# Linear attention and a gated MLP on one core: num of two pairs moved ahead, pair 0's 1/den spread alone, batch 2's transposes cut in four

## The chip, the cores and the metric

One core of a Trainium2 chip runs one program. The metric is device time in microseconds (us), as the median of a few executions. "Before" was run again in each set of experiments, on the same chip as the runs it is compared with; its median went from 302.92 to 303.43 us over five such sets, so differences of 0.3 us are read from traces, not from the times.

## The reference, cut to what matters

```python
def phi(x):
    return np.where(x > 0, x, np.exp(x) - 1.0) + 1.0
q_p, k_p = (phi(q), phi(k))                        # q, k, v: 8 batches, 8 heads, 576, 64
kv  = np.einsum('bhsd,bhse->bhde', k_p, v)
z   = np.sum(k_p, axis=2)
num = np.einsum('bhsd,bhde->bhse', q_p, kv)
den = np.einsum('bhsd,bhd->bhs', q_p, z)[..., None] + 1e-06
x   = num / den          # as 4608 tokens of 512
h   = x @ w_in           # 512 -> 2048
out = (h - np.tanh(h)) @ w_out
```

## The kernel before

Heads go in four pairs (two to the 128 partitions). The attention of batch b makes 576 tokens of x; the MLP works in nine tiles of 512 tokens, each a first layer (16 blocks of four 128x512 matmuls, each followed by tanh on ScalarE, ACT, and a subtraction on VectorE, DVE) and a second layer (16 steps of four). The attention of the next batches is put between these blocks, as little functions hung on block numbers (`s1` for the first layer, `s2` for the second). Batch 0 has nothing to hide behind. PSUM, where the tensor engine (PE) writes, is eight banks, handed out in a fixed rotation.

Names in the code and the profile lines: kp and qp are phi(k) and phi(q), qT is qp transposed; kz is kv times a mask, with the columns of z beside it; ns is num in SBUF (its "tail" is the last of the nine 64-token blocks of all pairs), rden is 1/den, and "spreading" means bringing rden to all 128 partitions; th is tanh(h), gT is h - th. "Dense" matmuls are those of the MLP.

The code is abridged; the last line is in words.

```python
def a_qT_pe(b, i, banks):                     # nine transposes of q, two banks, two copies
    ...
    for n, (j0, j1) in enumerate(((0, 5), (5, 9))):
        ps = banks()...
        for j in range(j0, j1):
            nc.tensor.transpose(ps[:, j - j0, :], ..., ident)
        if n == 0: nc.scalar.copy(dst, src)
        else:      nc.vector.tensor_copy(dst, src)

def a_num_copy(b, banks):                     # num to SBUF: the tail, then the pairs
    ns = rpool.tile(...)
    ps = num_mm(b, NP, banks)
    nc.scalar.copy(ns[:, :, 8, :], ps[:, 0:NP, :])
    if b == 0:
        for p in range(NP):
            num_mm(b, p, banks)
        for p in (0, 2):                      # two double copies
            nc.scalar.copy(ns[:, p:p + 2, 0:8, :]..., ps_all[:, 4 + p:6 + p, :])
    ...

# batch 0
a_qT_pe(0, 0, side); a_kv_half(0, 0, kvb)     # side: banks 4-7, kvb: banks 0-3
a_qT_pe(0, 1, side); a_kv_half(0, 1, kvb)
a_den(0, Banks([0]))                          # den on PE, 1/den on DVE
ns0 = a_num_copy(0, Banks([1, 4, 5, 6, 7]))
bp_a = a_spread_pe(0, 0, (0, 1))              # 1/den to 128 partitions, banks 0-3
bp_b = a_spread_pe(0, 4, (2, 3))              # banks 4-7
for p in range(NP):
    a_scale(0, p, ns0, (bp_a, bp_b)[p // 2], 144 * (p % 2))     # xT = num * (1/den)

# tile 0, second layer; tile 1, first layer (attn: banks 6, 7)
s2[14].append(lambda: a_qphi(2, 0)); s2[15].append(lambda: a_qphi(2, 1))
s1[1].append(lambda: a_kphi(2, 0))
s1[3].append(lambda: (a_kphi(2, 1), load_k(3), load_q(3)))
s1[5].append(lambda: a_qT_pe(2, 0, attn)); s1[7].append(lambda: a_qT_pe(2, 1, attn))
s1[9]: a_kv(2, attn)    s1[10]: load_v(4)    s1[11]: a_den, a_spread (1/den through DRAM: ds, then rdb)
```

## Time and profile before

| | before |
|---|---|
| time, median of 3 (then of 4) | 303.05 (302.92) us |
| span of the profiled execution | 301.5 us |
| TensorE (PE) busy | 97% |
| first dense matmul of tile 0 | 20.06 us |
| PE's waits at batch 2's transposes | 0.6 + 1.1 us |

As long as PE, busy for 97% of the time, is given the same work, the kernel gets faster only where PE stands still. The list of waits says where: in the chain of batch 0 before 20.06 us, and near 62 us. The lines are in the prediction.

### The profile page before, as it was taken

To read this page: it belongs to the slowest core of one execution; us is meant where nothing else is said; L and a number is where in the kernel's file an instruction comes from. 1 tells how busy PE (TensorE), PEld (TensorE's weight loads), DVE (VectorE), ACT (ScalarE), POOL (GpSimd) and SP (SyncE) were. 2 spreads that over 40 slices of the span, in tenths; PEclk is the share of its full clock that TensorE was granted. 3 is DMA by queue.
4 is the path that set the end of the run, shared out by engine and by line. 5 is a ranking of instruction groups with operands and counts; after the bars stand their busy time and mean duration, and the time that the engine had idled before them with its cause. 6 is when DMAs were issued, how large, how long until landed. Compare 5 with 4: busy or idle time off the path is not lost.

```text
span 301.5 us, 4703 instructions
## 1 busy us (share of the span) xinstructions
PE 292.2 (97%) x1790; PEld 138.7 (46%) x1790; DVE 180.0 (60%) x304; ACT 149.6 (50%) x228; POOL 51.7 (17%) x91
## 2 busy tenths in 40 slices
PE   8989999979999999999999999999999999999993
PEld 3544454444445444544454445444544444444441
DVE  7658944887557854785478556865681467008500
ACT  3637914954735653566256625662562166136420
POOL 8863253051006000600050003000000000000000
PEclk9999999999999999999999999999999999999998
DMA  6999999677879776967787777477108310130033
GB/s 95 193 206 206 205 207 206 171 113 139 214 101 188 147 170 139 152 109 200 142 145 128 192 149 125 85 177 148 38 2 193 71 35 0 37 86 18 2 70 70
DMA packets 36406, 38.23 MB, mean 127 GB/s; under 512 B 14432, under 2 KB 31008, under 8 KB 35616
## 3 DMA queue, kind: packets, MB, share of 16 engines
q0 software_dynamic: 17600, 18.35, 37.7%
q1 hardware_dynamic: 18784, 19.58, 28.9%
q8 instruction: 14, 0.23, 0.3%
q14 instruction: 8, 0.07, 0.1%
HBM read 43.78 MB, written 9.55 MB: 177 GB/s over the span
## 4 chain that ended last, share of the span: by engine, by line
PE 86%; DMA 4%; DVE 3%; ACT 2%; POOL 1%; issue 1%; SPq 0%; DVEq 0%; ACTq 0%; POOLq 0%
PE ps_all L275 39%; PE ps_all L290 38%; PE ps_all L165 4%; DMA out_dram<-osb 2%; PE ps_all L220 2%; DMA qraw<-in_q_dram 2%; ACT e L127 1%; DVE gT L281 1%; PE ps_all L190 1%; ACT osb L295 1%; PE ps_all L152 1%; POOL kraw L85 1%; PE ps_all L263 1%; DVE qp L129 1%; DVE kp L129 1%
## 5 line engine op out<-in xcount | busy, mean ns | idle before, releaser
L290 PE MATMUL ps_all<-w_out_sb,gT 128*128 128x512 bf16 x576 | 131.6, 379 | 0.0
L281 DVE TENSOR_TENSOR gT<-ps_all,th 128x512 bf16<-128x512 f32 x144 | 96.9, 687 | 53.6 <-ACT th L280 53.2
L275 PE MATMUL ps_all<-xT,w_in_sb 128*128 128x512 bf16 x576 | 128.2, 379 | 0.3 <-DVE xT L268 0.3
L280 ACT ACTIVATE th<-ps_all 128x512 f32<-128x512 f32 x144 | 85.2, 599 | 51.5 <-PE ps_all L275 46.8
L275 PEld LDWEIGHTS <-w_in_sb 128*128 128x128 bf16 x576 | 55.3, 98 | 66.6 <-issue 1.3
L290 PEld LDWEIGHTS <-gT 128*128 128x128 bf16 x576 | 55.6, 98 | 65.7 <-issue 0.3
L295 ACT COPY osb<-ps_all 128x512 f32<-128x512 f32 x36 | 21.1, 587 | 79.7 <-PE ps_all L290 59.6
L231 DVE TENSOR_TENSOR xT<-ps_all,rdb 128x512 bf16<-128x512 f32 x24 | 16.4, 689 | 11.8 <-PE ps_all L220 11.8
L104 POOL DMA_DIRECT2D v<-in_v_dram x32 | 19.2, 616 | 19.0 <-PE ps_all L165 6.0
L127 ACT ACTIVATE e<-kraw 128x1152 bf16<-128x1152 bf16 x16 | 18.5, 1165 | 5.3 <-DMA kraw<-in_k_dram 5.3
L129 DVE TENSOR_TENSOR kp<-e,r 128x1152 bf16<-128x1152 bf16 x16 | 12.2, 760 | 14.1 <-ACT e L127 13.0
L127 ACT ACTIVATE e<-qraw 128x1152 bf16<-128x1152 bf16 x16 | 18.4, 1166 | 0.6 <-DMA qraw<-in_q_dram 0.6
L129 DVE TENSOR_TENSOR qp<-e,r 128x1152 bf16<-128x1152 bf16 x16 | 12.1, 758 | 7.8 <-ACT e L127 7.0
L286 POOL COPY g<-gT 1x1 bf16<-1x1 bf16 x4 | 0.7, 176 | 92.9 <-DVE gT L281 92.9
L165 PE MATMUL ps_all<-v,kp 64*128 64x192 bf16 x288 | 13.7, 243 | 0.0
L165 PEld LDWEIGHTS <-kp 64*128 64x128 bf16 x288 | 11.5, 94 | 3.3 <-issue 2.5
L343 PE MATMUL ps_all<-zero 128*128 128x512 bf16 x36 | 10.3, 460 | 1.2 <-DVE zero L302 1.2
L220 PE MATMUL ps_all<-qT,kz 128*128 128x512 bf16 x32 | 11.2, 379 | 0.0
L89 POOL DMA_DIRECT2D kraw<-in_k_dram x14 | 8.7, 628 | 11.0 <-ACT th L280 9.6
L89 POOL DMA_DIRECT2D qraw<-in_q_dram x14 | 8.8, 642 | 6.1 <-DVE r L128 6.1
L268 DVE TENSOR_TENSOR xT<-ns,ps_all 128x576 bf16<-128x576 f32 x8 | 5.6, 749 | 5.2 <-PE ps_all L263 5.2
L174 DVE TENSOR_TENSOR kz<-ps_all,mask 128x320 bf16<-128x320 f32 x14 | 6.2, 486 | 3.7 <-PE ps_all L165 3.7
(46 smaller groups left out, 92.3 us busy)
## 6 DMA issues: line engine op xcount, KB each, us to landing
out_dram<-osb SPq DMA_DIRECT2D x72, 128.0 KB
rdb<-ds SPq DMA_DIRECT2D x12, 576.0 KB
v<-in_v_dram POOLq DMA_DIRECT2D x32, 144.0 KB, 6.4
kraw<-in_k_dram POOLq DMA_DIRECT2D x14, 288.0 KB, 5.1
qraw<-in_q_dram POOLq DMA_DIRECT2D x14, 288.0 KB, 7.0
w_in_sb<-in_moe_w_in_dram POOLq DMA_DIRECT2D x4, 512.0 KB, 10.1
w_out_sb<-in_moe_w_out_dram POOLq DMA_DIRECT2D x4, 512.0 KB, 13.2
kraw<-in_k_dram POOLq DMA_DIRECT2D x4, 144.0 KB, 3.7
```

The lines of the kernel that those rows point to most:

```text
L89: nc.gpsimd.dma_start(out=t[64 * hg:64 * hg + 64].rearrange("p i h j d -> p (i h) (j d)"), in_=src[b, 4 * hg:4 * hg + 4].rearrange("h (p j ...
L104: nc.gpsimd.dma_start(out=v_b[b % 2][64 * hg:64 * hg + 64, i, 0:2].rearrange("p h j d -> p h (j d)"), in_=v[b, h0:h0 + 2].rearrange("h (p ...
L127: nc.scalar.activation(e, x, AF.Exp)
L129: nc.vector.tensor_tensor(store[b][:, i].rearrange("p j h d -> p h j d"), e, r, ALU.min)
L165: nc.tensor.matmul(ps[hg], kp[r, i, j].rearrange("p h d -> p (h d)"), vt[r, i, :, j, :], start=(j == 0), stop=(j == J - 1))
L220: nc.tensor.matmul(ps, kz[:, p // 2, p % 2, 0:128], qT[:, p % 2, 0:8, p // 2, :], start=True, stop=True)
L231: nc.vector.tensor_mul(xT[:, p, S * b:S * b + 512].rearrange("p (j t c) -> p j t c", j=8, t=4), ps.rearrange("p j (t c) -> p j t c", t=4), ...
L275: nc.tensor.matmul(h, w_in_sb[:, p, fi * 128:(fi + 1) * 128], xT[:, p, c * 512:(c + 1) * 512], start=(p == 0), stop=(p == NP - 1))
L280: nc.scalar.activation(th, h, AF.Tanh)
L281: nc.vector.tensor_sub(gT[:, fi, :], h, th)
L290: nc.tensor.matmul(o, gT[:, fi, i * 128:(i + 1) * 128], w_out_sb[:, fi, :], start=(fi == 0), stop=(fi == NF - 1))
L295: nc.scalar.copy(osb, o)
```

## The change

Its intent: let ACT copy out half of batch 0's num early, let the first dense matmul wait for one scaled pair instead of two, and let the transposes of batch 2 flow between blocks instead of standing in a queue for two banks. The core of the diff (cut: num of batch 1, only rewritten in the same order, and the helpers):

```diff
     a_qT_pe(0, 1, side)
+    ns0 = new_ns(0)
+    for p in (0, 2):
+        a_num_copy(0, ns0, p, side)
     a_kv_half(0, 1, kvb)
     a_den(0, Banks([0]))
-    ns0 = a_num_copy(0, Banks([1, 4, 5, 6, 7]))
-    bp_a = a_spread_pe(0, 0, (0, 1))
-    bp_b = a_spread_pe(0, 4, (2, 3))
+    a_num_copy(0, ns0, NP, Banks([1]))
+    for p in (1, 3):
+        a_num_copy(0, ns0, p, side)
+    bp_a = a_spread_pe(0, 0, (0,))
+    bp_b = a_spread_pe(0, 4, (1, 2, 3))
     for p in range(NP):
-        a_scale(0, p, ns0, (bp_a, bp_b)[p // 2], 144 * (p % 2))
+        a_scale(0, p, ns0, bp_b if p else bp_a, 144 * (p - 1) if p else 0)
 ...
-            s1[5].append(lambda: a_qT_pe(2, 0, attn))
-            s1[7].append(lambda: a_qT_pe(2, 1, attn))
+            for n in range(4):
+                s1[4 + n].append(lambda n=n: a_qT_pe(2, n // 2, attn, (n % 2,)))
```

More of the change, by code (lines that the diff above doesn't have):

```diff
@@ L144, in a_qT_dma, with a_qT_pe @@
             in_=qp_t[b].rearrange("p i j h d -> p (i j h d)"))
-    def a_qT_pe(b, i, banks):
-        if i == 0:
+    def a_qT_pe(b, i, banks, parts=(0, 1)):
+        if i == 0 and 0 in parts:
             new_qT(b)
-        for n, (j0, j1) in enumerate(((0, 5), (5, 9))):
+        for n in parts:
+            j0, j1 = ((0, 5), (5, 9))[n]
             ps = banks().bitcast(BF16).rearrange("p (j t) -> p j t", t=128)
@@ L238, in a_num, with new_ns, a_num_copy @@
                 ps[:, 0:NP, :].rearrange("p a (t c) -> p a t c", t=4), rdb[:, :, :, 8, :])
-    def a_num_copy(b, banks):
-        ns = rpool.tile([128, NP, J, 64], F32, name="ns", tag="rdb")
-        ps = num_mm(b, NP, banks)
-        nc.scalar.copy(ns[:, :, 8, :], ps[:, 0:NP, :])
-        if b == 0:
-            for p in range(NP):
-                num_mm(b, p, banks)
-            for p in (0, 2):
-                nc.scalar.copy(ns[:, p:p + 2, 0:8, :].rearrange("p a j t -> p a (j t)"),
-                               ps_all[:, 4 + p:6 + p, :])
-        else:
-            for p in range(NP):
-                ps = num_mm(b, p, banks)
-                nc.scalar.copy(ns[:, p, 0:8, :], ps)
-        return ns
+    def new_ns(b):
+        return rpool.tile([128, NP, J, 64], F32, name="ns", tag="rdb")
+    def a_num_copy(b, ns, p, banks):
+        ps = num_mm(b, p, banks)
+        if p < NP:
+            nc.scalar.copy(ns[:, p, 0:8, :], ps)
+        else:
+            nc.scalar.copy(ns[:, :, 8, :], ps[:, 0:NP, :])
     def a_spread_pe(b, bank0, pairs):
@@ L384, with num1 @@
             s2[8].append(lambda: a_den(1, side))
-            s2[9].append(lambda: (sub.update(ns=a_num_copy(1, side)), load_v(3)))
+            def num1():
+                sub["ns"] = new_ns(1)
+                for p in (NP, 0, 1, 2, 3):
+                    a_num_copy(1, sub["ns"], p, side)
+                load_v(3)
+            s2[9].append(num1)
             s2[11].append(lambda: spread1(0))
```

## The prediction

> **What bounds the kernel now.** I read the page first: one busy engine, no throttling (the clock row is 9 throughout until the last slice), nothing slow in a row.
>
> ```profile
> PE 292.2 (97%) x1790; PEld 138.7 (46%) x1790; DVE 180.0 (60%) x304; ACT 149.6 (50%) x228; POOL 51.7 (17%) x91
> ```
>
> The tensor engine (PE) is nearly always occupied, so only stretches where PE waits, or runs ahead of what it needs, can give time back. The second view was therefore the list of who waits for whom, for PE alone (us in total, times, longest):
>
> ```profile
> PE ps_all L152 <- DVE qT L158: 1.1, 1, 1.1
> PE ps_all L152 <- ACT qT L156: 0.6, 1, 0.6
> ...
> PE ps_all L275 <- DVE xT L268: 0.3, 1, 0.3
> PE ps_all L263 <- ACT ns L249: 0.3, 1, 0.3
> PE ps_all L263 <- DVE rden L201: 0.2, 1, 0.2
> PE ps_all L190 <- DVE kz L182: 0.2, 1, 0.2
> ```
>
> The last four belong to the start (batch 0, before the first L275 matmul), the first two to batch 2's transposes near 62 us. The change touches exactly these two places. Everything else in PE's order is untouched. So I read the timeline of both. The start, PE and then DVE (start, length in us):
>
> ```profile
> 14.41 0.94 PE L165 MATMUL ps_all<-v,kp 64*128 64x192 bf16 x18
> 15.27 0.31 PE L190 MATMUL ps_all<-qT,kz 128*32 128x144 bf16 x8
> 15.74 0.48 PE L190 MATMUL ps_all<-qT,kz 128*32 128x144 bf16 x8 [0.16 <-DVE kz L182]
> 16.05 0.24 PE L194 MATMUL ps_all<-one,eps 128*32 128x144 bf16 x4
> ...
> 17.54 1.13 PE L263 MATMUL ps_all<-rden,sel 32*128 32x144 f32 x20 [0.17 <-DVE rden L201]
> 18.95 0.76 PE L263 MATMUL ps_all<-rden,sel 32*128 32x144 f32 x12 [0.28 <-ACT ns L249]
> 20.06 4.26 PE L275 MATMUL ps_all<-xT,w_in_sb 128*128 128x512 bf16 x19 [0.34 <-DVE xT L268]
> ```
>
> ```profile
> 16.33 1.06 DVE L201 RECIPROCAL rden<-ps_all 128x144 f32<-128x144 f32 x1 [0.42 <-PE ps_all L194]
> 18.59 2.75 DVE L268 TENSOR_TENSOR xT<-ns,ps_all 128x576 bf16<-128x576 f32 x4 [1.19 <-PE ps_all L263]
> ```
>
> To be seen: a strictly serial chain, kv (L165), mask, den (L190, L194), reciprocal, spread of 1/den (L263), scale (L268), first L275 matmul at 20.06. The first L275 waits for two scales, not one: its banks 0 to 3 hold the spread of pairs 0 and 1.
>
> Third, what follows. PE is dense from 20.06 to 60.9, with one tiny break inside a row of equal matmuls: consecutive L290 matmuls start 0.216 apart, but the seventeenth starts 0.266 after the sixteenth, at 37.37. It is the first that reads the second quarter of w_out.
>
> ```profile
> 37.37 0.53 PEld L290 LDWEIGHTS <-gT 128*128 128x128 bf16 x3 [0.17 <-issue]
> ```
> ```profile
> 20.29 0.75 POOL L114 DMA_DIRECT2D w_out_sb<-in_moe_w_out_dram x1 [0.62 <-DMA w_in_sb<-in_moe_w_in_dram]
> ```
> ```profile
> DMA to landing us min/median/max: 11.6/13.2/17.0
> ```
>
> That quarter was issued at 20.29 and needed the 17.0 us, so it landed at 37.3 (the landing records say 37.33), 0.04 before that matmul starts. The DMA view of 10 to 38 us shows 9 tenths in every slice and about 203 GB/s. So the transfer, which does not depend on PE, is already just on the path there.
>
> **What the Trainium skill says.** "TensorEngine Tiling (Array Packing)", Key Properties: different tiles run weight loads and matmuls in parallel. The trace agrees for the spread: its four 32-row groups each start one pass every 0.122 us side by side, so eight matmuls do not cost twice four in full. "DMA: Bandwidth & Descriptors", Issuing engines are not separate DMA queues: all transfers share the same 16 DMA engines and interleave. The trace agrees: w_out's second quarter competes with w_in, q, k and v of batch 1 and takes 17.0 us. "Perfetto Trace Analysis", Optimization Strategy: in the regime of interest find the engine's gaps and the semaphore that ends each. That is the procedure here.
>
> **The change part by part.**
>
> (a) Num of pairs 0 and 2 ahead of kv's second half. Two 128x512 matmuls, 0.216 us start to start in the trace, now lie ahead of L165 at 14.41. The kz and qT they read are ready (masks end 14.17 and 14.40), so at most a hair of waiting. Den and the reciprocal come after kv, so this puts about +0.38 us on the chain (2 x 0.216, less 0.05 of the hop that was there). What it buys is on ACT: two copies (taken as 0.59 each from the 128x512 copies of L295) run at 14.9 to 16.0, where ACT was idle, instead of after 17. The other two then end near 18.4 (tail copy from 16.92, then two more), where the double copies ended at 18.90.
>
> (b) Spread of pair 0 alone. The last pass of eight matmuls starts at 18.19; of the first four, at 17.94. Gain 0.245. Scale 0 moves from 18.59 to 18.59 + 0.38 - 0.245 = 18.72.
>
> (c) First L275 waits for scale 0 only. Scales start 0.67 apart, so one scale less: the first L275 comes at 20.06 + 0.38 - 0.245 - 0.67 = 19.52.
>
> (d) Price of (b): twelve matmuls in the second spread. In the built instruction order of the changed kernel scale 1 waits for PE and scales 2 and 3 don't: the wait is for the whole second spread, pairs 1 to 3. Its fourth matmul needs bank 7, copied out at 18.43, so from 18.49 the last row group has six passes: 0.23 for the first, then 0.122 each, last start 19.22, end 19.50, scale 1 at about 19.6. Scale 0 ends near 19.47, so DVE loses 0.2. Scale 1 ends at 20.36; PE, with four matmuls per pair (0.86), wants pair 1 at 20.38. No stall. Sum for the start: PE ahead by 0.5 us.
>
> (e) Is this 0.5 us kept? By 37.37 no. PE would reach w_out's second quarter at about 36.8, the transfer still lands at 37.33 (its issue waits for other landings only, not for PE). PE then stands 0.5 us where it stood 0.05. Kept: 0.05. The third quarter (42.3) and fourth (45.7) land over 1 and 3 us before they are needed.
>
> (f) Transposes of batch 2 in four pieces: no instruction more or less. The view of 58.5 to 63.8 us:
>
> ```profile
> 60.88 0.75 ACT L156 COPY qT<-ps_all 128x640 bf16<-128x640 bf16 x1
> ...
> 61.59 1.28 DVE L281 TENSOR_TENSOR gT<-ps_all,th 128x512 bf16<-128x512 f32 x2
> ...
> 61.68 0.44 PE L152 MATMUL ps_all<-ident,qp 128*128 128x128 bf16 x5 [0.61 <-ACT qT L156]
> ...
> 62.79 0.41 DVE L158 COPY qT<-ps_all 128x512 bf16<-128x512 bf16 x1
> ...
> 63.25 0.38 PE L152 MATMUL ps_all<-ident,qp 128*128 128x128 bf16 x4 [1.13 <-DVE qT L158]
> ```
>
> Five and then four transposes wait for banks 6 and 7, emptied by ACT and DVE. By start times PE loses 0.78 + 1.29 = 2.07 us. Split up, ACT's copy stands one tanh earlier: it starts at 60.4, ends about 61.1, and PE, which now comes there at 60.05, goes on at 61.2, does five transposes and one more block of L275 (0.28 + 0.86) and at 62.35 comes to the last four. These still need DVE's copy, which keeps its place in DVE's order (the orders of the two kernels agree on DVE), behind the same two subtractions. DVE runs back to back from 56.05, so the copy still ends at 63.20. PE has done the same work when it passes 63.25. Saved: 0; the same 2 us of waiting are only divided otherwise (1.1 for ACT, 0.9 for DVE). The tanh put behind ACT's copy ends near 61.7, before DVE wants it at 62.19.
>
> Batch 1's num is only rewritten, in the same order: 0. Sum: 303.05 - 0.05 - 0 = 303.0.
>
> **The rivals.**
> 1. The 0.5 us of the start is kept, giving 302.5. For it: landing varies between executions, the run under the profiler took 303.31 against a median of 303.05, so w_out may land earlier without it. Against: PE is within 0.05 us of the landing, and a saturated stretch has no reason to run faster.
> 2. Spreading the transposes removes most of the 2.07 us, giving 301.0 to 301.5. For it: that is plainly the intent, and two waits are named there. Against: DVE's unbroken row up to the copy, and its unchanged order. Only if ACT's earlier copy let DVE catch up would it work, and DVE waits for nothing there.
> 3. The added matmuls and the longer second spread cost more than assumed (scale 1 after 20.0, a stall in the second group of L275): 303.0 to 303.3, as the transfer absorbs nothing of a loss beyond 0.05.
>
> **Range and chances.** I give my sum two thirds, rival 1 a quarter, the others the rest. Weighted: 0.65 x 303.0 + 0.25 x 302.5 + 0.05 x 301.3 + 0.05 x 303.2 = 302.8. With the spread of the runs of before (302.71 to 303.22) the range is 302.2 to 303.3. Two per cent is 6 us, three times the largest wait touched: faster 0.01, same 0.98, slower 0.01.
>
> **What would show it.** Right: first L275 at 19.4 to 19.7; the reciprocal about 0.38 later than 16.33; scale 1 about 0.2 after scale 0's end; a wait of about 0.5 us before the seventeenth L290, still at 37.3 to 37.4; near 62 us a wait of 0.9 to 1.1 us on ACT and of 0.7 to 0.9 on DVE, with the last four transposes still near 63.25. Wrong: L290's seventeenth matmul before 37.0 (rival 1), DVE's copy for batch 2 before 62.5 relative to the same L275 start (rival 2), or the first L275 no earlier than 20.0 (rival 3).

## The result, and the profile after

The changed kernel took 302.98 us (302.79 to 303.41, 4 runs), the kernel before 302.92 (302.71 to 303.22, 4 runs). The ratio is 1.0003 with a 95% interval of 0.9986 to 1.002. (Ratios are computed as the mean time of one kernel's runs over that of the other's runs of the same rounds, so they are not quite the ratio of the medians.) Nothing was gained. The spans of the two profiled executions differ by 0.2 us, 301.5 and 301.3.

The list of waits of PE after (us in total, times, longest):

```profile
PE ps_all L153 <- ACT qT L157: 1.0, 1, 1.0
PE ps_all L153 <- DVE qT L159: 0.7, 1, 0.7
...
PE ps_all L258 <- DVE rden L202: 0.6, 1, 0.6
PE ps_all L270 <- DVE xT L263: 0.2, 1, 0.2
PE ps_all L191 <- DVE kz L183: 0.2, 1, 0.2
```

At the transposes (L153) 0.6 and 1.1 us have become 1.0 and 0.7: the same 1.7, divided otherwise. In the start PE now waits 0.6 us for the reciprocal (L202), 0.2 before, because it has less to do there.

The timeline of the start after, PE and then DVE (start, length in us; lines are numbered five lower or one higher than before):

```profile
14.61 0.62 PE L221 MATMUL ps_all<-qT,kz 128*128 128x512 bf16 x2
15.16 0.92 PE L166 MATMUL ps_all<-v,kp 64*128 64x192 bf16 x18
...
16.49 0.47 PE L191 MATMUL ps_all<-qT,kz 128*32 128x144 bf16 x8 [0.17 <-DVE kz L183]
...
18.28 1.40 PE L258 MATMUL ps_all<-rden,sel 32*128 32x144 f32 x32 [0.60 <-DVE rden L202]
19.89 4.48 PE L270 MATMUL ps_all<-xT,w_in_sb 128*128 128x512 bf16 x20 [0.21 <-DVE xT L263]
```
```profile
17.08 1.06 DVE L202 RECIPROCAL rden<-ps_all 128x144 f32<-128x144 f32 x1 [0.42 <-PE ps_all L195]
19.08 2.79 DVE L263 TENSOR_TENSOR xT<-ns,ps_all 128x576 bf16<-128x576 f32 x4 [0.95 <-PE ps_all L258]
```

The reciprocal starts 0.75 us later than before (17.08 against 16.33). From there to the first dense matmul it is 2.81 us instead of 3.72 (19.89 - 17.08, 20.06 - 16.33; the differences are of unrounded times). So 0.91 us was gained behind the reciprocal, and 0.75 lost ahead of it.

The end of the transposes' stretch after:

```profile
60.19 0.74 ACT L157 COPY qT<-ps_all 128x640 bf16<-128x640 bf16 x1
...
60.98 0.44 PE L153 MATMUL ps_all<-ident,qp 128*128 128x128 bf16 x5 [0.99 <-ACT qT L157]
...
61.37 1.28 DVE L276 TENSOR_TENSOR gT<-ps_all,th 128x512 bf16<-128x512 f32 x2
...
62.57 0.41 DVE L159 COPY qT<-ps_all 128x512 bf16<-128x512 bf16 x1
...
63.03 0.38 PE L153 MATMUL ps_all<-ident,qp 128*128 128x128 bf16 x4 [0.75 <-DVE qT L159]
```

ACT's copy now stands ahead of one tanh and PE goes on earlier, but the last four transposes start when DVE's copy ends, as before. Counted from the first dense matmul of tile 1 (called F: 53.50 before, 53.28 after) they start at F+9.75 in both kernels.

### The profile page after: what moved, and what is told of

Read it like the earlier page. It is cut to its first block, busy times and chain, and to the rows that moved or that the text cites. A ratio compares the mean times of both kernels' runs of the same rounds, so it can differ in the third digit from the quotient of the medians.

```text
span 301.3 us, 4706 instructions
## 1 busy us (share of the span) xinstructions
PE 291.9 (97%) x1790; PEld 138.3 (46%) x1790; DVE 180.2 (60%) x304; ACT 149.6 (50%) x230; POOL 52.1 (17%) x91
## 4 chain that ended last, share of the span: by engine, by line
PE 79%; DMA 9%; DVE 5%; ACT 2%; issue 1%; POOL 1%; SPq 0%; DVEq 0%; POOLq 0%; ACTq 0%
PE ps_all L270 38%; PE ps_all L285 33%; DMA qraw<-in_q_dram 4%; PE ps_all L166 4%; DMA out_dram<-osb 2%; DVE gT L276 2%; PE ps_all L221 2%; DMA v<-in_v_dram 2%; ACT e L127 1%; ACT osb L290 1%; DVE kp L129 1%; PE ps_all L191 1%; POOL kraw L85 1%; DVE r L128 1%; DVE qp L129 1%
## 5 line engine op out<-in xcount | busy, mean ns | idle before, releaser
L285 PE MATMUL ps_all<-w_out_sb,gT 128*128 128x512 bf16 x576 | 131.6, 379 | 0.0
L275 ACT ACTIVATE th<-ps_all 128x512 f32<-128x512 f32 x144 | 85.3, 600 | 51.7 <-PE ps_all L270 47.2
L285 PEld LDWEIGHTS <-gT 128*128 128x128 bf16 x576 | 55.5, 98 | 65.7 <-issue 0.2
L290 ACT COPY osb<-ps_all 128x512 f32<-128x512 f32 x36 | 21.1, 586 | 79.6 <-PE ps_all L285 59.5
```

What stands on the lines that cost most here:

```text
L275: nc.scalar.activation(th, h, AF.Tanh)
L285: nc.tensor.matmul(o, gT[:, fi, i * 128:(i + 1) * 128], w_out_sb[:, fi, :], start=(fi == 0), stop=(fi == NF - 1))
L290: nc.scalar.copy(osb, o)
```

## The experiments

Twelve runs, all with a correct result. T is the start of the first transpose of batch 0; it depends on when q lands, and moved between 11.4 and 12.4 us. F is the start of the first dense matmul of tile 1. The diffs are abridged; the expectation quoted below each says on which kernel it was made.

### num_only: part (a) by itself, and once more

```diff
-    bp_a = a_spread_pe(0, 0, (0,))          # spread and transposes set back to before
+    bp_a = a_spread_pe(0, 0, (0, 1))
```

> Only part (a): num of pairs 0 and 2 ahead of kv's second half, four single copies; spread and transposes as before. Times are counted from the first transpose (T), because the landing of q moves T by 0.1 us between executions; before: reciprocal T+4.20, first L275-type matmul T+7.93. My theory: the two matmuls and one hop cost 0.51 us on the chain (the profile after showed this, I had said 0.38), and nothing is gained, because the first dense matmul still waits for scales 0 and 1: reciprocal T+4.7, first dense matmul T+8.4 to T+8.5, so about 0.4 to 0.5 us slower than before (303.3 to 303.5, inside noise by the clock alone). Rival: num ahead is the useful part, ACT's copies come out of the way and the first dense matmul comes before T+7.8.

304.73 us against 303.42, ratio 1.0045 (1.0021 to 1.007). The reciprocal came at T+4.68, the first dense matmul at T+8.37 (before: T+4.21, T+7.93). The price of about 0.45 us and the missing gain are as expected, the total was not. PE's list of waits has

```profile
PE ps_all L270 <- DVE xT L263: 1.1, 1, 1.1
```

against 0.3 before, and two more things happened in some executions: a wait for the spread 1/den of batch 2 (0.8 us on DVE; this tile is called rdb), and a fall of the granted clock (the share of full speed at which PE was let run). So it was run again:

> The run with num alone once more. Its first profile showed 0.4 us more up to F and 0.5 us more in tile 1, where the spread 1/den of batch 2 landed at 83.25, just after its use was due. If the latter was chance: 0.4 to 0.6 us above the kernel before this time, the interval reaching below 1.003, and no wait for rdb in the profile. If num alone brings it on: again over 1.2 us above, with that wait.

303.59 against 303.27, ratio 0.9997 (0.996 to 1.0034): the executions were 305.02, 303.32, 302.94 and 303.85. The profiled one was the slowest. It had no wait for rdb, and the view of stretches shows what it had instead (window, length, then busy time of PE, PEld, DVE, ACT, POOL, the granted clock, DMA share and GB/s):

```profile
20.00:21.00 1.00, 0.86 (x3) 0.39 (x3) 1.00 (x3) 0.00 (x0) 0.27 (x1) 0.66 1.24 204
21.00:22.00 1.00, 1.00 (x4) 0.29 (x2) 0.42 (x1) 0.00 (x0) 0.48 (x1) 0.50 1.24 208
```

After the wait of 1.1 us before the first dense matmul the clock was granted at one half from about 20.3 to 23.7 us (worked out from the shares of these windows and of the one from 23 to 24, which had 0.63), and tile 0's first layer took 15.50 us (20.14 to 35.64) instead of 13.81 (20.06 to 33.87). The first run of the same kernel had the same wait and full clock in its profile; two others of its executions had a mean clock of 0.994, as this one. So num alone cost about 0.45 us in the first profile and 0.55 in the second (first dense matmul at T+8.37 and T+8.48, before T+7.93), and 1.7 more where the clock fell. Neither expectation for the total held: the 1.2 us were not there every time, and they had two causes.

### spread_only: part (b) by itself

```diff
-    bp_a = a_spread_pe(0, 0, (0, 1))
-    bp_b = a_spread_pe(0, 4, (2, 3))
+    bp_a = a_spread_pe(0, 0, (0,))
+    bp_b = a_spread_pe(0, 4, (1, 2, 3))
```

> Only part (b): pair 0 spread alone, num and copies as before. My theory: first dense matmul 0.9 us earlier (T+7.0: 0.245 for four matmuls fewer, 0.67 for one scale fewer), but the second spread still has to wait for ACT's double copy (end 18.90), its twelve matmuls end about 1 us after that, and scale 1 comes 0.9 us after scale 0's end; so PE stalls about 0.8 us between the fourth and the fifth dense matmul, and the fifth comes at T+8.6 to T+8.8 (before: T+7.93+0.86 = T+8.79). Net gain 0 to 0.2 us. Rival, the plain sum: no stall, fifth dense matmul at T+7.9, gain 0.9 us.

303.09 against 303.42, ratio 0.9991 (0.9966 to 1.0016). Timeline of PE, then of DVE:

```profile
17.68 1.01 PE L263 MATMUL ps_all<-rden,sel 32*128 32x144 f32 x12 [0.17 <-DVE rden L201]
19.09 1.00 PE L263 MATMUL ps_all<-rden,sel 32*128 32x144 f32 x20 [0.40 <-ACT ns L249]
20.03 4.17 PE L275 MATMUL ps_all<-xT,w_in_sb 128*128 128x512 bf16 x17
```
```profile
18.48 0.75 DVE L268 TENSOR_TENSOR xT<-ns,ps_all 128x576 bf16<-128x576 f32 x1 [0.95 <-PE ps_all L263]
20.21 2.08 DVE L268 TENSOR_TENSOR xT<-ns,ps_all 128x576 bf16<-128x576 f32 x3 [0.98 <-PE ps_all L263]
```

Scale 0 is done at 19.23, yet the first dense matmul is at 20.03. I had expected it at T+7.0 with a stall behind the fourth; it came at T+7.78. I had overlooked that PE issues in order: the second spread stands ahead of the dense matmuls, and waits for ACT's double copy. The net gain by F is 0.06 us (F - T is 41.31, before 41.37), as expected, and the place of the stall was wrong. (This trace lacks some matmul records, so the fifth dense one cannot be named.) Scale 1 waits 0.98 us for the second spread. The two parts need each other: b alone has no copies in time for the second spread, a alone pays for copies that nothing uses.

### pieces_only: part (f) by itself

```diff
-            s1[5].append(lambda: a_qT_pe(2, 0, attn))
-            s1[7].append(lambda: a_qT_pe(2, 1, attn))
+            for n in range(4):
+                s1[4 + n].append(lambda n=n: a_qT_pe(2, n // 2, attn, (n % 2,)))
```

> Only part (f): batch 2's transposes in four pieces, the start as before. Counted from the first dense matmul of tile 1 (F, 53.50 before): the last four transposes came at F+9.75 before. My theory: DVE's queue sets this, so F+9.7 to F+9.8 again, with the two waits 1.0 and 0.75 us in the view of waits instead of 0.6 and 1.1; time same as before within 0.1 us. Rival (the split removes the wait): F+9.2 or less, 0.5 us or more saved.

303.57 against 303.42, ratio 1.0006 (0.9986 to 1.0025). The last four transposes: F+9.75; the waits: 1.0 and 0.8 us. As expected, cutting them is worth nothing by itself.

### q_early: take away DVE's backlog

```diff
-            s2[14].append(lambda: a_qphi(2, 0))
-            s2[15].append(lambda: a_qphi(2, 1))
+            s2[11].append(lambda: a_qphi(2, 0))
+            s2[13].append(lambda: a_qphi(2, 1))
```

> The changed kernel, and in addition the exp and min of q of batch 2 are put three and two steps earlier in tile 0's second layer (after steps 11 and 13 instead of 14 and 15), where ACT sits idle for 1.9 us. No instruction more or less. My theory (DVE's backlog, begun by the two q-phi at the end of tile 0, holds the copy that the last transposes wait for): DVE's row before the copy starts 1.5 to 1.8 us earlier, the last four transposes come at about F+8.0 to F+8.4 instead of F+9.75, the two waits of 1.0 and 0.75 us shrink to under 0.4 together, and the kernel takes 1.3 to 1.8 us less: about 301.3. Rival (bank order or ACT's copies hold the transposes): the waits stay at 1.7 us together and the time at 303.

301.73 against 303.42, ratio 0.9948 (0.9932 to 0.9963), with the changed kernel's start. The last four transposes came at F+8.49, 1.26 us earlier. The wait for ACT's copy is gone, the one for DVE's remains:

```profile
PE ps_all L153 <- DVE qT L159: 0.5, 1, 0.5
```

That is a little over the 0.4 expected; the transposes came 0.1 us later than F+8.0 to F+8.4, and the time is 0.4 above "about 301.3", though the 1.7 us below the kernel before are in the range. The rival of banks falls: their order was not touched. That of ACT does not fall here, since the early q takes two exp from ACT's queue too; k_split, below, moves work of DVE alone. (In this profile PE also lost 0.2 us at w_out's second quarter: it landed at 36.89, and the seventeenth matmul came at 36.93, 0.42 after the sixteenth.)

The same two lines were then put into the kernel before:

> The kernel before, with nothing of the change, but with the two q-phi of batch 2 after steps 11 and 13. If cutting the transposes in four is worth nothing even when the backlog is smaller (my theory, as DVE's copy still ends last): last four transposes at F+8.4 to F+8.6, as with the cut ones (F+8.49), and the time some 0.35 us (the start) above that of the early q on the changed kernel: about 302.0. Rival (the pieces count once the backlog is gone): F+8.9 or later.

301.61 against 303.27, ratio 0.9939 (0.991 to 0.9968), last four transposes at F+8.49 again. So the pieces are worth nothing here either. The 0.35 us that the start should have cost did not show in the time; in this profile q had landed early (T at 11.45).

### k_late and k_split: the other way to shorten DVE's queue

```diff
-            s1[3].append(lambda: (a_kphi(2, 1), load_k(3), load_q(3)))
+            s1[6].append(lambda: (a_kphi(2, 1), load_k(3), load_q(3)))
```

> The changed kernel, with the second k-phi of batch 2 (exp on ACT, two instructions on DVE) moved from after block 3 to after block 6 of tile 1, so that 1.2 us of DVE work stand behind instead of ahead of the copy that the last four transposes wait for. If DVE's queue is what holds them (my theory): last four transposes at F+8.4 to F+8.7 (F = first dense matmul of tile 1) instead of F+9.75, and 1.0 to 1.3 us less than the changed kernel on the same chip. Rival (it was ACT's side that the early q relieved, or the phase of the q loads): F+9.3 or later, under 0.4 us.

306.16 against 303.27, ratio 1.0087 (1.0056 to 1.0117): slower, while the transposes did just what was expected (F+8.52). The list of waits and PE's timeline name the new place:

```profile
PE ps_all L221 <- DVE xT L232: 2.4, 1, 2.4
```
```profile
84.43 0.38 PE L221 MATMUL ps_all<-qT,kz 128*128 128x512 bf16 x1 [2.43 <-DVE xT L232]
```

The num of batch 2 needs 1/den spread by a round trip through DRAM. Its issues on the SP queue:

```profile
69.97 1.33 SPq L209 DMA_DIRECT2D ds<-rden  x4
75.23 1.12 SPq L212 DMA_DIRECT2D rdb<-ds  x2
```

The second waits for the first to land: 5.26 us, where the kernel before had 2.43 (71.47 to 73.90). The loads of k, q and v for batches 3 and 4, issued later and closer together here, landed up to 74.88 by the trace's landing records, and the four small writes (4.5 KB each) up to 75.08, right behind them. In the trace's DMA packets the first write moved only at 73.29, 3.3 us after its issue; in the kernel before it was 0.8 us (71.47 to 72.27). After PE's wait the clock was at 0.50 from about 85.1 to 88.5 us (shares of 0.78, 0.50 and 0.86 in the windows 84 to 86, 86 to 88 and 88 to 90), which adds to the loss.

To tell the load's delay from the k-phi's, only the last DVE instruction of the k-phi was moved:

```diff
-            s1[3].append(lambda: (a_kphi(2, 1), load_k(3), load_q(3)))
+            s1[3].append(lambda: (late.update(kp=phi_parts(2, k_t, kp_t, 1)), load_k(3), load_q(3)))
+            s1[6].append(lambda: late["kp"]())          # the min alone
```

> The changed kernel with only the last DVE step of the second k-phi (the min, 0.6 us of DVE's row) moved from block 3 to block 6 of tile 1; its exp and max stay, so the loads of k and q of batch 3 leave when they did. The late k-phi had won 1.2 us at the transposes and lost 2.4 us where the num of batch 2 waited for the spread 1/den, whose landing the delayed loads had run into. If that reading is right: last four transposes at F+9.1 to F+9.3, no wait of over 0.8 us for rdb, and 0.4 to 0.7 us less than the changed kernel, 302.2 to 302.5. If moving the k-phi itself did the harm: rdb waited for again by 2 us or more, 304 or more.

302.81 against 303.43, ratio 0.998 (0.9955 to 1.0004). Last four transposes at F+9.25 and a wait of 0.7 us for rdb, as expected:

```profile
62.12 0.38 PE L165 MATMUL ps_all<-ident,qp 128*128 128x128 bf16 x4 [0.25 <-DVE qT L171]
```

Only an instruction of DVE had been moved, so it is DVE's queue that holds them. The time is 0.3 us above what I had said, though 0.6 below the kernel before of the same set, with an interval that reaches past 1. From kv of batch 2 to kv of batch 3 it was 27.92 us instead of 27.32: the gain at the transposes was given back at rdb. The loads of k and q left when they did against F (F+7.83, changed kernel F+7.84); that of v, which waits for kv of batch 2, left 0.4 us earlier.

### after_again: how far executions differ

> The changed kernel once more, for the spread between executions: first dense matmul of tile 0 at T+7.5 to T+7.65, F at T+41.0, last four transposes F+9.75; the landing of w_out's second quarter anywhere from 35.9 to 37.4 (seen so far over six profiles); time within 0.3 us of the kernel before. If my step on a fixed landing at 37.3 were right, the landing would be there again.

302.88 against 303.27, ratio 0.9982 (0.995 to 1.0015). T+7.57 and F+9.75 as expected. The landing records of w_out's second quarter end at 36.18 here; over all 14 profiles of this case they range from 35.70 to 37.33, and the kernel before had the latest. This is no matter of the change: the programs of before, pieces_only and q_early_whole are the same up to then, and theirs were 37.33, 36.26 and 35.70.

### q_early_4_7, den_first, v_late: the pieces put together

These build on each other, from q_early on. First the transposes whole again, the first half one block earlier than before, so that DVE's first copy stands behind one subtraction less:

```diff
-            for n in range(4):
-                s1[4 + n].append(lambda n=n: a_qT_pe(2, n // 2, attn, (n % 2,)))
+            s1[4].append(lambda: a_qT_pe(2, 0, attn))
+            s1[7].append(lambda: a_qT_pe(2, 1, attn))
```

> The early q on the changed kernel, and batch 2's transposes whole again, after blocks 4 and 7: DVE's copy of the first half then stands behind four subtractions and not five (0.6 us earlier), which the cut did not bring about. Theory (position in DVE's queue decides): last four transposes at F+7.9 to F+8.1 instead of F+8.49, the wait of 0.5 us for DVE's copy gone, 0.3 to 0.5 us less than the early q: 301.2 to 301.4. Rival (nothing more to have there, or another wait comes in): F+8.4 or later.

301.49 (300.79 to 302.2) against 303.43, ratio 0.9942 (0.9919 to 0.9965). Last four transposes at F+7.89, no wait there at all. The time is 0.1 us above the range I had given. In the profiled execution the second quarter of w_out landed at 37.32, and PE, which was early, stood there:

```profile
37.36 1.02 PE L285 MATMUL ps_all<-w_out_sb,gT 128*128 128x512 bf16 x4 [0.68 <-DMA w_out_sb<-in_moe_w_out_dram]
```

This is the very wait of step (e) of the prediction. And DVE waited 1.4 us in two waits for rdb.

Then the start without num on the chain:

```diff
-    for p in (0, 2):
-        a_num_copy(0, ns0, p, side)
     a_kv_half(0, 1, kvb)
     a_den(0, Banks([0]))
-    a_num_copy(0, ns0, NP, Banks([1]))
-    for p in (1, 3):
-        a_num_copy(0, ns0, p, side)
+    for p, bk in ((NP, Banks([1])), (0, side), (2, side), (1, side)):
+        a_num_copy(0, ns0, p, bk)
+    nc.vector.tensor_copy(ns0[:, 3, 0:8, :], num_mm(0, 3, side))
```

> The same as the one with transposes after blocks 4 and 7, and the start rebuilt: num of all pairs behind den again (PE idles there during the reciprocal), pair 3's copy on DVE after the reciprocal, spread of pair 0 alone kept. If the two num matmuls on the chain were the price I saw: reciprocal back at T+4.2 to T+4.3 (changed kernel T+4.7 to T+4.8; T as far as v has landed by then), first dense matmul at T+7.2 to T+7.4, fifth at T+8.3 to T+8.4 (changed kernel T+8.43 to T+8.49, before T+8.79): 0 to 0.2 us less than its sister run. Rival: copies on ACT come too late without the early num (bank 6 free at 18.6) and the fifth comes at T+8.6 or later.

301.36 (301.22 to 301.46) against 303.43, ratio 0.9937 (0.9923 to 0.9952). The chain could not be judged from T here: q had landed early (11.37) and PE then waited 0.4 us for v. From the reciprocal to the first dense matmul it was 3.03 us (changed kernel 2.81), and DVE waited 1.6 us for rdb in two waits, 1.2 the longer.

At last the load that nobody needs for long was taken out of rdb's way:

```diff
-                s1[10].append(lambda: load_v(c + 3))
+                if c == 1:
+                    s2[10].append(lambda: (gate(xT[:, :, S * n1:S * n1 + 1], 0), load_v(c + 3)))
+                else:
+                    s1[10].append(lambda: load_v(c + 3))
```

> The rebuilt start with the early q and the transposes after blocks 4 and 7, and the load of v of batch 4, which nothing needs before tile 3, held back (by a one-element POOL copy) until the first num of batch 2 is scaled. Theory: the write of 1/den of batch 2 (ds) sat in the DMA engines behind the loads of k, q and v that leave in the same 10 us, so the spread (rdb) was issued 3.4 us after it (2.4 in the kernel before) and the num of batch 2 waited, 1.2 us on DVE; without v in the way rdb is issued under 2.4 us after ds, no wait for rdb, kv of batch 3 comes 27.3 us after kv of batch 2 (28.3 in the sister run, 27.3 before), and the kernel takes 0.7 to 1.0 us less than the sister: 300.3 to 300.7. Rival (other transfers hold it, or v comes too late for batch 4): the wait stays, or a new one of v in tile 3 appears, and the time is 301.2 or more.

300.79 (300.62 to 301.5, 5 runs) against 303.24, ratio 0.9918 (0.9904 to 0.9931). This beats the kernel before by some 2.4 us (0.8%), and so the changed one, which is level with it. On the SP queue:

```profile
69.00 1.34 SPq L209 DMA_DIRECT2D ds<-rden  x4
71.42 1.12 SPq L212 DMA_DIRECT2D rdb<-ds  x2
```

2.42 us from issue to issue, no wait for rdb left, and kv of batch 3 came 27.38 us after kv of batch 2 (28.30 in den_first). The gain over den_first is 0.6 us by the medians (0.4 if each median is taken against that of the kernel before in its own set), less than the 0.7 to 1.0 expected and 0.1 outside the range for the time. And the trace does not show that the load of v was what held the write: before, after and num_again had the same 2.42 to 2.43 us with that load in place, and one program run twice gave 2.43 and 3.10 (after, after_again). One profile with a short wait is what the theory foretells, but chance would give it too. In the profiled execution, the slowest of the five, another transfer took part of it:

```profile
PE ps_all L191 <- DMA qT<-qp: 0.6, 1, 0.6
```

This is the transpose by DMA of a later batch, which none of the other profiles waited for. It was issued at 82.19, among the four moved loads of v (80.77 to 82.53), and landed 12.9 us later by its semaphore; in the 13 other profiles, where these loads were elsewhere, that took 6.0 to 6.3 us. So the moved load very likely brought it on, and part of what v_late gained in one place it paid in another. With T at 11.97 and no wait for v, this run also gives the verdict on the start that den_first could not: reciprocal at T+4.29, first dense matmul at T+7.32, the fifth at T+8.32; in the changed kernel's two profiles T+4.82 and T+4.76, T+7.63 and T+7.57, T+8.49 and T+8.43. Those 0.1 to 0.2 us are as expected.

## Why the prediction was right, and where its steps were not

The time (302.8 predicted, 302.98 measured) and "same" held. The reason for the transposes was right. For the start, the small net effect was right by luck: the gain was put too high (0.5 us), and so was the loss at the transfer that was to take 0.45 of it, which did not come; the two errors nearly cancel. Of the five signs that the prediction named for being right, only that of the transposes came true: the first L275 was not at 19.4 to 19.7 but at 19.89, the reciprocal not 0.38 but 0.75 later, scale 1 followed scale 0 without a gap, and there was no wait before the seventeenth L290. By its steps:

- **(a), num ahead of kv: right mechanism, mis-sized.** I said +0.38; in the profile after it was 0.51, and num_only shows about 0.45 with nothing in return. The term that failed is "2 x 0.216, less 0.05 of the hop that was there". The hop was not saved: from the second transposes to kv's second half it is 0.61 us before, and 1.04 in the seven other profiles with num ahead, so 0.43, the two matmuls in full. The profile after (1.12) had 0.08 on top.
- **The rest of the delay of 0.75 was not in the sum.** T was 0.13 later (q landed later), and the second transposes another 0.11, behind a max on DVE (L128) that took 1.00 us where the kernel before showed 0.70. The same instruction takes 0.45 later in the kernel, where POOL is idle; at that time POOL was issuing a DMA and then clearing `sel`. Over all profiles the max took 0.91 to 1.26 us in the four in which this clearing began while it ran (after, after_again, pieces_only, q_early_whole), and 0.51 to 0.83 in the ten others. That the two engines get in each other's way is still a guess: no run here took POOL's work away, and a max that lasts longer for another reason would also meet the clearing more often.
- **(b) and (c): right to 0.01 us.** 0.245 + 0.67 = 0.915 us less between reciprocal and first dense matmul; measured 0.91 (0.91 in after_again too). That the first dense matmul had to wait for scale 1 at all, although it needs pair 0 only, is a matter of banks. The Trainium skill says in "PSUM — Partial Sum Buffer", PSUM bank collisions raise a hardware error, that accesses are to be guarded by bank, not by address. The trace before agrees: scale 1 read banks 0 to 3 until 20.00, and the first dense matmul, which writes bank 0, started at 20.06.
- **(d): right in kind, smaller.** Scale 1 started 0.71 us after scale 0; before it was 0.67, and 0.88 was foretold (18.72 to 19.6). The second spread ran without a break, since everything came 0.37 us later than foretold and the copies were out by then (at 18.63). There was no stall in the second group.
- **So the sum for the start was 0.5 and measured 0.17** (20.06 to 19.89). Counted from T, which the change does not touch, it is 0.30 (T+7.93 to T+7.63; T+7.57 in after_again).
- **(e), the transfer that takes the gain: wrong as a fixed wall.** In the profile after, w_out's second quarter landed at 36.23, not 37.33; the seventeenth L285 matmul started at 37.15, 0.216 after the sixteenth, without a wait. The 0.17 us of the start and the 0.05 us of that wait were kept up to F (53.28 against 53.50) and to the span's end (301.3 against 301.5). I had read one execution's landing as if the kernel fixed it; it moves by 1.6 us among profiles whose programs are the same up to then. The wait itself is real: it came (0.68 us) in the profile of q_early_4_7, where PE was early and the landing late, and in that of q_early (0.2 us).
- **(f), the transposes: right, by its own reasons.** The view of waits has 1.0 and 0.7 us, against the foretold 0.9 to 1.1 and 0.7 to 0.9; last transposes at F+9.75 in both, alone (pieces_only) as together. That DVE's queue is what holds them was argued in the prediction; the experiments show it: shorten the queue by another route and the four transposes come 1.26 (q_early), 1.23 (k_late), 0.50 (k_split) and 1.86 us (q_early_4_7) earlier. In k_split nothing but a DVE instruction was moved.
- **The rivals.** The kept start (302.5) is true of its mechanism, but there were only 0.2 to 0.3 us to keep. The big gain at the transposes did not happen. The stall in the second group did not happen.

So the expected gain of the change went in two ways: at the start, half of the 0.91 us was paid for by the two matmuls that make it possible (0.43 to 0.51), and more in this profile by q's later landing and the longer max; at the transposes there was none, since the cut moved ACT's copy and not DVE's. What is left, 0.2 to 0.3 us, is under the spread of the runs. Two things stay open: what makes the landings of w_out and of rdb move between executions, and whether the loads are what delays the small write of 1/den. k_late and v_late fit that, but the same write took 2.43 us beside the loads in the kernel before.

## What to carry to other kernels

When an engine waits for two others in turn, find which of the two queues is full without a gap: only shortening that one moves the end, and relieving the other just turns one wait into a longer other. Before putting work ahead of a serial chain, look whether the same engine idles later in that chain; there it may cost nothing (the reciprocal came at T+4.21 before, T+4.29 in v_late and T+4.76 to T+4.82 in the changed kernel). And after each gain on the busy engine look at the transfers due next: they land when they land, differently in each execution, and a gain can be lost there (here to w_out's second quarter and to the spread of 1/den).

## What the Trainium skill lacked or had wrong

- "TensorE: Matmul & The Clock Gate", Why this matters for your kernels, advises no gaps of PE of over about 3 us. Here a wait of 1.1 us, with lightly used stretches ahead of it, was followed by a clock of 0.50 for about 3.4 us (num_again), which cost 1.7 us; the same wait in num_only's profile was not. After the wait of 2.4 us in k_late the clock was at 0.50 for as long. So keeping every gap under the figure of the page is not enough to be safe. The same page, A second HAM failure mode: psum-queue depth-cycling, does tell of short idles that make the clock swing; what it lacks is how long they are.
- "DMA: Bandwidth & Descriptors", Queues, rings and completion order, says that each DMA engine takes turns between its queues packet by packet. What no page that I read gives is how long a small write takes beside a row of loads on another queue, and it is far from fixed: from the issue of the first of four writes of 4.5 KB to that of the transfer that waits for them it took 2.42 to 5.26 us over the 14 profiles, 2.43 and 3.10 in two of the same program. The longest is that of k_late, where the loads of k and q were issued latest; in q_early the writes were through (72.36) before the last load had landed (72.67), so they do not always wait for the end of the row.
- No page that I read says how much landings differ between executions: w_out's second quarter landed anywhere from 35.70 to 37.33 us over 14 profiles, and at 37.33, 36.26 and 35.70 in three whose programs are the same up to then.
